# A kernel's planner learns of the port that VectorE and GpSimd share, and its loads are reordered

## Chip, cores and metric

One core of a Trainium2 chip runs the kernel. The metric is the device time of one execution in microseconds, the median of several runs on the same chip. Five engines work side by side and only semaphores order them: TensorE (PE in the profile; PEld is its weight load), VectorE (DVE), ScalarE (ACT), GpSimd (POOL), and SyncE (SP), which issues the DMA transfers.

## Reference

Three stages follow one another, all with float32 results. The attention has two batches of 8 heads, 576 positions and 64 dimensions; half of the heads look at the 32 positions before, the other half at every 32nd position. Its output, 1152 tokens of 512, goes through an MLP with a squared relu, whose weights come as float64, and then through four experts that are all computed and summed by weight.

```python
def _attn_ref(q, k, v):
    scores = scale * np.matmul(q, k.transpose(0, 1, 3, 2))
    mask_local = (rel >= 0) & (rel < stride)
    mask_strided = (rel >= 0) & (pos[None, :] % stride == pos[:, None] % stride)
    scores = np.where(masks[None, :, :, :], scores, -1000000000.0)
    attn = np.exp(scores - np.max(scores, axis=-1, keepdims=True))
    attn = attn / (np.sum(attn, axis=-1, keepdims=True) + 1e-09)
    return np.matmul(attn, v).astype(np.float32)

def _moe_ref(x, w_in, w_out):          # 512 -> 2048 -> 512
    h = np.maximum(x @ w_in, 0.0)
    return (h * h @ w_out).astype(np.float32)

def _moe2_ref(x, domain_probs, w1, w2):   # four experts, 512 -> 1024 -> 512
    p = domain_probs / (domain_probs.sum(-1, keepdims=True) + 1e-09)
    for e in range(E):
        out += p[:, e:e + 1] * (np.maximum(x @ w1[e], 0.0) @ w2[e])
```

## The kernel before

Products are made in three passes: each operand is split into a rounded upper part (ACT copies it, "hi") and a lower part (the difference, "lo"), and PE adds upper times upper, upper times lower and lower times upper (mm3, lines 617 to 619).

**Attention** works in 16 groups: six strided ones (lines 354 to 384) and ten local ones (lines 420 to 452). attend() gives each the same chain: loads of k, q and v by SP; scores on PE (L363 and L367, or L430 to L438); the maximum on DVE (L485); for local groups a negation (L492) and up to four exponentials on ACT with their sums (L490), for strided ones a subtraction (L495), one exponential (L496) and a sum (L497); then L498 and L499 on DVE; the normalisation on POOL (L500); transposes on PE (L372 or L442); a copy on ACT (L480); values on PE (L384 or L452); the x tile's upper part on ACT (L509) and its lower part on DVE (L513). Six groups form the startup, seven come "second", three "third". Local groups fill the first half of an x tile's 512 features, strided ones the second.

**The MLP** runs in 48 steps over three blocks of 384 tokens, 128 hidden features a step. A step's first products come in four quarters (features in the order 2, 3, 0, 1), so the first two need the strided groups alone. ACT and DVE make relu, square and the two parts (L650 to L660); two steps later the second products follow. The first eight steps take block 0, the next eight block 1.

**Weights** of this MLP arrive as float64, in 16 units of two halves (512 KB each, L568). ACT scales the upper words (L575), DVE shifts (L580), puts in the sign (L584) and the low bits (L589), ACT makes the upper part (L595), POOL the lower (L599). Expert weights are float32 and need only L595 and L599, the latter on DVE. The **experts** fill the span from about 240 us on; some products are combined so that seven stand for eight, and POOL builds sums of weights for that (L776 to L788).

**What orders the work** is Plan (class at the top). Each task names its engine with a cost in ns, what it follows, a rank, and buffers that it takes from rings and frees. run() plays the program through with these costs: an engine that falls idle takes the ready task of lowest rank whose buffers are there. What comes out is one fixed order for every engine and for SP's loads; on the chip each engine goes through its list and waits by semaphores. Ranks are counted in ns: due(n) for a step of the MLP, less CONV for the conversion of weights first used there, less FETCH for their load; for attention a start plus R_MAX, R_EXP, R_NORM, R_T, R_V, R_X along the chain. When PE has nothing before its first MLP task, it multiplies zeros (warm, L961). The rings are small: 3 raw weights, 2 of each middle tile, 10 finished units, 4 each of q, k and v, 3 of p.

```python
    def pool(n):
        return int(n * 2.05) + 190
    def dma(nbytes):
        return int(nbytes / 357) + 60
            lo_engines = {"pool": pool(n)} if wide_ else {"dve": dve(n)}
            t = plan.add(lo_engines, lo, after=[t], rank=rank + R_LO, ...)
```

Of the kernel before, what the change touches and what calls it, by code (L numbers as in the profile page):

```python
# [16 lines left out]
P = 128  # L17
# [22 lines left out]
class Plan:  # L40
# [7 lines left out]

    SAME, CROSS, DMA = 100, 200, 2200
# [13 lines left out]
    def add(self, engines, emit, after=(), rank=0, take=(), free=(), adds=(), behind=None, quiet=False, tenses=(), relaxes=()):  # L63
# [5 lines left out]
        t.quiet, t.tenses, t.relaxes = quiet, tenses, relaxes  # L69
        self.tasks.append(t)  # L70
        return t

    def run(self):
# [21 lines left out]
        while done < len(self.tasks):  # L95
# [25 lines left out]
            for e in ready:  # L121
                while idle[e] and ready[e]:
                    held, got = [], None
                    while ready[e]:
# [20 lines left out]
                    order.append((now, len(order), got.emit, e))  # L145
                    push(got.end, "end", got)
# [15 lines left out]
def tile_attention_mlp_experts(ctx: ExitStack, tc: tile.TileContext, a, out):  # L162
# [48 lines left out]
    NP = 3  # L211
    NQ = 4
    NPT = 2
# [25 lines left out]
    plan.ring("v", many(at, "v", NQ, [P, 512]))  # L239
# [12 lines left out]
    def mm_r(n):  # L252
        return int(n / 2.4) + 3

    def mm_s(n):
        return int(n / 2.4) + 13
# [9 lines left out]

    def dma(nbytes):
        return int(nbytes / 357) + 60
# [17 lines left out]
    IN, IN7, OUT = 3 * KD * mm_s(TB), 42 * mm_s(TB), 9 * mm_s(DM)  # L286
# [172 lines left out]
    attention_done = []  # L459

    def attend(g, rank, rings):
# [3 lines left out]
        for what, nbytes in zip("kqv", g.bytes):  # L465
            loads.append(plan.add({"dma": dma(nbytes)}, lambda e, w=what: g.load(env, w), rank=rank - 5000, take=[(env, what, [what])]))
# [17 lines left out]
        t = plan.add({"pe": g.cost_s}, lambda e: g.scores(env), after=[t_cb, t_go, *loads[:2]], rank=rank, take=[(env, "S", rings)], free=[(env, "q"), (env, "k")])  # L484
        t = plan.add({"dve": dve(n)}, lambda e: nc.vector.tensor_reduce(out=stat(0), in_=view(env["S"], g.cols), op=ALU.max, axis=AX.X), after=[t], rank=rank + R_MAX, take=[(env, "st", ["st"])])  # L485
        if g.units <= 4:
# [5 lines left out]
            t = plan.add({"dve": 90}, lambda e: nc.vector.tensor_scalar(out=stat(0), in0=stat(0), scalar1=-SCALE, scalar2=None, op0=ALU.mult), after=[t], rank=rank + R_MAX + 300)  # L492
            t = plan.add({"act": g.units * 317}, each, after=[t], rank=rank + R_EXP, take=[(env, "p", ["p"])], free=[(env, "S")])
# [4 lines left out]
        t = plan.add({"dve": 80}, lambda e: nc.vector.tensor_scalar(out=stat(1), in0=stat(1), scalar1=1e-9, scalar2=None, op0=ALU.add), after=[t], rank=rank + R_EXP + 1000)  # L498
# [23 lines left out]
    for k, g in enumerate(startup):  # L522
        attend(g, BASE + EACH * k, ["bank_a", "bank_y"])
    second = [Local(0, 3), Local(0, 4)] + [Strided(1, j) for j in range(3)] + [Local(1, 0), Local(1, 1)]
    for k, g in enumerate(second):
        attend(g, START - AHEAD + k * (due(half) - START - END2) // len(second), ["bank_a"])
    third = [Local(1, j) for j in (2, 3, 4)]
    for k, g in enumerate(third):
        attend(g, due(half) - AHEAD + k * (due(2 * half) - due(half) - END3) // len(third), ["bank_a"])
# [26 lines left out]
    for u in sorted(when, key=lambda x: when[x]):  # L556
# [4 lines left out]
        rank = when[u] - (CONV0 if soon else CONV)  # L561
        for j in range(2):
# [41 lines left out]
            if wide_:  # L604
                t = plan.add({"act": act(n)}, small, after=[t], rank=rank, take=[(env, "mid", ["mid"])])
                t = plan.add({"dve": dve(n // 2)}, shift, after=[t], rank=rank + 500, take=[(env, "val", ["val"])])
                t = plan.add({"dve": dve(n)}, sign, after=[t], rank=rank + 700, free=[(env, "mid")])
                t = plan.add({"dve": dve(n)}, low, after=[t], rank=rank + 1200, free=[(env, "raw")])
            t = plan.add({"act": act(n)}, hi, after=[t, chain["w"]], rank=rank + 2000, take=[(w_env[u], "w", ["w"])] if j == 0 else [], quiet=not wide_)
# [441 lines left out]
```

## Time and profile before

| | us |
|---|---|
| runs of the kernel (3): median, lowest, highest | 647.59, 647.18, 648.01 |
| profiled execution: time, span from first to last instruction | 647.54, 645.8 |
| PE busy, share of span | 631.5, 98% |
| VectorE busy | 360.8, 56% |
| ScalarE busy | 235.6, 36% |
| GpSimd busy | 105.9, 16% |
| granted TensorE clock, mean | 0.997 |

A span is cut into stretches and engines are compared within one; shares of the whole span mix a crowded beginning with a long stretch in which only PE matters. A matmul's time in a row is its latency; matmuls follow one another at about half of it. "Idle before" is time in which that engine stood still until the named one released it.

### The profile page before, as it was taken

Reading aid. Unit: us, or ns where it says so; the run is one execution under the profiler, and the core shown is the slowest. Engines: PE = TensorE matmul, PEld = TensorE weight load, DVE = VectorE, ACT = ScalarE, POOL = GpSimd, SP = SyncE. Lnnn points to the kernel's source line nnn. Section 1 sums busy time; section 2 is a strip of 40 time slices with the busy share of each in tenths; the row PEclk is TensorE's granted clock in tenths of the full one; section 3 lists DMA queues with packets and bytes.
Section 4 is the critical chain, followed back from the end, with each engine's and each line's share of the span. In section 5 each row is a group of like instructions: output and inputs, shape, how many; then the busy total and the mean of one; then the engine's idle time right before and its main releaser. Section 6 shows DMA issues by size and latency. Waiting matters only on the chain.

```text
span 645.8 us, 9891 instructions
## 1 busy us (share of the span) xinstructions
PE 631.5 (98%) x3868; PEld 580.2 (90%) x3868; DVE 360.8 (56%) x664; ACT 235.6 (36%) x527; POOL 105.9 (16%) x119
## 2 busy tenths in 40 slices
PE   7998999999999999999999999999999999999997
PEld 4777889999999999999999999999999999999997
DVE  4898886288623264945557415557324557643512
ACT  2956675354423244522333312333212333321110
POOL 2435341033100000030112000113001012400000
PEclk9998999999999999999999999999999999999999
DMA  8976434034300023231133301123301222100201
GB/s 276 265 228 179 150 127 131 0 100 145 98 1 1 1 65 98 72 91 38 38 94 136 89 1 50 63 90 110 81 1 50 81 82 97 33 2 0 98 2 49
DMA packets 28990, 53.51 MB, mean 83 GB/s; under 512 B 4432, under 2 KB 10000, under 8 KB 28944
## 3 DMA queue, kind: packets, MB, share of 16 engines
q1 hardware_dynamic: 28944, 52.89, 26.7%
q8 instruction: 30, 0.49, 0.3%
q14 instruction: 16, 0.13, 0.1%
HBM read 50.52 MB, written 2.36 MB: 82 GB/s over the span
## 4 chain that ended last, share of the span: by engine, by line
PE 88%; DVE 5%; ACT 2%; DMA 2%; issue 1%; POOL 1%; SPq 1%; DVEq 0%; ACTq 0%; POOLq 0%
PE bh L617 14%; PE bh L618 14%; PE bh L619 14%; PE by L835 8%; PE by L836 8%; PE by L834 8%; PE by L617 5%; PE by L619 4%; PE by L618 4%; PE ba L836 2%; PE ba L835 2%; PE ba L834 2%; DVE val L580 1%; DVE val L589 1%; DVE val L584 1%
## 5 line engine op out<-in xcount | busy, mean ns | idle before, releaser
L617 PE MATMUL bh<-x,w 128*128 128x384 f32 x416 | 141.8, 341 | 1.7 <-DVE h L660 1.7
L619 PE MATMUL bh<-x,w 128*128 128x384 f32 x416 | 139.8, 336 | 0.0
L618 PE MATMUL bh<-x,w 128*128 128x384 f32 x416 | 139.7, 336 | 0.0
L872 DVE TENSOR_TENSOR c<-bh,c 128x384 f32<-128x384 f32 x80 | 43.1, 556 | 85.9 <-ACT c L885 58.4
L836 PE MATMUL by<-w,h 128*128 128x512 f32 (+1 forms) x232 | 89.0, 384 | 0.0
L835 PE MATMUL by<-w,h 128*128 128x512 f32 (+1 forms) x232 | 89.0, 384 | 0.0
L834 PE MATMUL by<-w,h 128*128 128x512 f32 (+1 forms) x232 | 88.5, 382 | 0.0
L617 PEld LDWEIGHTS bh<-x,w 128*128 128x128 f32 x416 | 78.5, 189 | 4.7 <-DVE h L660 3.2
L618 PEld LDWEIGHTS bh<-x,w 128*128 128x128 f32 x416 | 78.5, 189 | 1.0
L619 PEld LDWEIGHTS bh<-x,w 128*128 128x128 f32 x416 | 78.4, 188 | 0.0
L779 POOL TENSOR_TENSOR sf<-raw 128x256 f32<-128x256 f32 x16 | 12.1, 755 | 347.1 <-DMA raw<-in_w_dram 283.8
L617 PE MATMUL by<-h,w 128*128 128x384 f32 x192 | 65.5, 341 | 0.3 <-ACT h L657 0.3
L618 PE MATMUL by<-h,w 128*128 128x384 f32 x192 | 64.5, 336 | 0.6 <-DVE h L660 0.6
L619 PE MATMUL by<-h,w 128*128 128x384 f32 x192 | 64.6, 336 | 0.0
L599 POOL TENSOR_TENSOR w<-val,w 128x512 fp32r<-128x512 f32 x32 | 43.3, 1361 | 76.4 <-ACT w L595 73.9
L654 DVE SCALAR_TENSOR_TENSOR bh<-bh,r 128x384 f32<-128x384 f32 x48 | 27.0, 562 | 51.0 <-ACT r L650 51.0
L929 DVE SCALAR_TENSOR_TENSOR h<-bh,h 128x384 fp32r<-128x384 f32 x32 | 17.8, 557 | 64.0 <-ACT h L926 64.0
L904 ACT ACTIVATE h<-c 128x384 fp32r<-128x384 f32 x64 | 31.8, 518 | 54.6 <-DVE c L872 34.5
L836 PEld LDWEIGHTS by<-w,h 128*128 128x128 f32 x232 | 43.6, 188 | 8.5
L834 PEld LDWEIGHTS by<-w,h 128*128 128x128 f32 x232 | 43.6, 188 | 8.0
L835 PEld LDWEIGHTS by<-w,h 128*128 128x128 f32 x232 | 43.6, 188 | 8.1
L599 DVE TENSOR_TENSOR w<-raw,w 128x512 fp32r<-128x512 f32 x64 | 43.1, 696 | 9.3 <-ACT w L595 9.3
(122 smaller groups left out, 1039.2 us busy)
## 6 DMA issues: line engine op xcount, KB each, us to landing
raw<-in_w_dram SPq DMA_DIRECT2D x64, 256.0 KB, 2.7
raw<-in_wi_dram SPq DMA_DIRECT2D x16, 512.0 KB, 3.7
raw<-in_wo_dram SPq DMA_DIRECT2D x16, 512.0 KB, 3.6
raw<-in_w_dram SPq DMA_DIRECT2D x16, 512.0 KB, 3.6
out_dram<-acc SPq DMA_DIRECT2D x8, 256.0 KB, 2.1
v<-in_vs_dram SPq DMA_DIRECT2D x6, 256.0 KB, 4.4
v<-in_vl_dram SPq DMA_DIRECT2D x8, 192.0 KB, 3.8
k<-in_kl_dram SPq DMA_DIRECT2D x8, 160.0 KB, 4.5
```

The lines of the kernel that those rows point to most:

```text
L599: eng[e].tensor_tensor(out=w[:, 1, cs], in0=value(), in1=f32(w[:, 0, cs]), op=ALU.subtract)
L617: nc.tensor.matmul(dst, lhsT=wh, rhs=xh, start=start, stop=False)
L618: nc.tensor.matmul(dst, lhsT=wh, rhs=xl, start=False, stop=False)
L619: nc.tensor.matmul(dst, lhsT=wl, rhs=xh, start=False, stop=stop)
L654: nc.vector.scalar_tensor_tensor(out=h, in0=h, scalar=0.0, in1=env["r"], op0=ALU.max, op1=ALU.mult)
L779: nc.gpsimd.tensor_tensor(out=got(env["sf"])[:, 0], in0=part(env, 1, 0), in1=part(env, 1, 1), op=ALU.add)
L834: nc.tensor.matmul(o, lhsT=h[:, 0, ts], rhs=w[:, 0], start=start, stop=False)
L835: nc.tensor.matmul(o, lhsT=h[:, 0, ts], rhs=w[:, 1], start=False, stop=False)
L836: nc.tensor.matmul(o, lhsT=h[:, 1, ts], rhs=w[:, 0], start=False, stop=stop)
L872: return lambda e: nc.vector.tensor_tensor(out=got(c[key]), in0=c[bank][:, :TB], in1=got(c[other]), op=ALU.add)
L904: nc.scalar.activation(out=env["hid"][:, 0], in_=got(c[key]), func=AF.Relu)
L929: nc.vector.scalar_tensor_tensor(out=env["hid"][:, 1], in0=env["H"][:, :TB], scalar=0.0, in1=f32(env["hid"][:, 0]), op0=ALU.max, op1=ALU.s ...
```

## The change

The planner gets a common mark for the port: a task with port=True, and every task on GpSimd, starts only when no such task is running by the plan. port=True is given to the DVE instructions L492, L498, L580, L584, L589, L599 and, in the later stages, to the differences and lower parts that read two tiles of the on-chip buffer. A float64 weight's lower part may go to GpSimd or VectorE. Costs are new: loads at 310 bytes per ns, PE's 384 columns at the higher of the two old figures, a normalisation of its own. Ranks are new throughout, CONV most of all, and the startup's loads get a lead of 9000 instead of 5000 while later groups get 1775. The rings of v and p grow. The two halves of a wi unit are loaded in the other order, and a quarter product waits for the half that it reads, not for both. Scores of the second and third groups follow the transposes of the group three before. In the expert stage the hold on GpSimd's sums ends later.

```diff
+        self.shared = 0
...
+        t.quiet, t.tenses, t.relaxes, t.port = quiet, tenses, relaxes, port
...
-                        if not (t.quiet and e in self.tense) and all(any(self.rings[r] for r in rings) for _, _, rings in t.take):
+                        if not (t.quiet and e in self.tense or (t.port or e == "pool") and now < self.shared) and all(any(self.rings[r] for r in rings) for _, _, rings in t.take):
...
+                    if got.port or e == "pool":
+                        self.shared = got.end
...
-    START, STEP, WITH, URGENT = 22863, 3902, 2300, 6004
+    START, STEP, WITH, URGENT = 16764, 7401, 1796, 5606
...
-    EACH = 3300
-    AHEAD = 4582
-    END2 = 7000
-    END3 = 12767
+    EACH = 3285
+    AHEAD = 3550
+    END2 = 5361
+    END3 = 11947
     CONV0 = 7431
-    CONV = 9000
-    FETCH = 2019
-    WITH2 = 1082
+    CONV = 70240
+    CONV2 = 9000
+    FETCH = 1560
+    WITH2 = 542
...
-    R_MAX = 1500
-    R_EXP = 2200
-    R_NORM = 6589
-    R_T = 6622
-    R_V = 4414
+    R_MAX = 2415
+    R_EXP = 1898
+    R_NORM = 1629
+    R_T = 1668
+    R_V = 5078
     R_X = 8089
-    R_LO = 2600
-    R_OUT = 1960
+    R_LO = 1232
+    R_OUT = 2590
...
-    NP = 3
+    NP = 5
     NQ = 4
+    NV = 6
+    LEAD0, LEAD = 9000, 1775
...
-    plan.ring("v", many(at, "v", NQ, [P, 512]))
+    plan.ring("v", many(at, "v", NV, [P, 512]))
...
     def mm_r(n):
-        return int(n / 2.4) + 3
-
-    def mm_s(n):
         return int(n / 2.4) + 13
...
+    def norm(n):
+        return int(n * 1.9) + 70
+
     def dma(nbytes):
-        return int(nbytes / 357) + 60
+        return int(nbytes / 310) + 60
...
-            loads.append(plan.add({"dma": dma(nbytes)}, lambda e, w=what: g.load(env, w), rank=rank - 5000, take=[(env, what, [what])]))
+            loads.append(plan.add({"dma": dma(nbytes)}, lambda e, w=what: g.load(env, w), rank=rank - lead, take=[(env, what, [what])]))
...
-        t = plan.add({"pe": g.cost_s}, lambda e: g.scores(env), after=[t_cb, t_go, *loads[:2]], rank=rank, take=[(env, "S", rings)], free=[(env, "q"), (env, "k")])
+        t = plan.add({"pe": g.cost_s}, lambda e: g.scores(env), after=[t_cb, t_go, *loads[:2], *(transposed[-3:-2] if len(rings) == 1 else [])], rank=rank, take=[(env, "S", rings)], free=[(env, "q"), (env, "k")])
...
-        t = plan.add({"pool": pool(n)}, lambda e: eng[e].tensor_tensor(out=view(env["p"]), in0=view(env["p"]), in1=wide(1), op=ALU.mult), after=[t], rank=rank + R_NORM, free=[(env, "st")])
+        t = plan.add({"pool": norm(n)}, lambda e: eng[e].tensor_tensor(out=view(env["p"]), in0=view(env["p"]), in1=wide(1), op=ALU.mult), after=[t], rank=rank + R_NORM, free=[(env, "st")])
         t = plan.add({"pe": g.cost_t}, lambda e: g.transposes(env), after=[t, t_ci], rank=rank + R_T, take=[(env, "T", rings)], free=[(env, "p")])
+        transposed.append(t)
...
-        rank = when[u] - (CONV0 if soon else CONV)
-        for j in range(2):
+        rank = when[u] - (CONV0 if soon else CONV if wide_ else CONV2)
+        for j in (1, 0) if kind == "wi" else (0, 1):
...
-                t = plan.add({"dve": dve(n // 2)}, shift, after=[t], rank=rank + 500, take=[(env, "val", ["val"])])
+                t = plan.add({"dve": dve(n // 2)}, shift, port=True, after=[t], rank=rank + 500, take=[(env, "val", ["val"])])
...
-            lo_engines = {"pool": pool(n)} if wide_ else {"dve": dve(n)}
-            t = plan.add(lo_engines, lo, after=[t], rank=rank + R_LO, free=[(env, "val") if wide_ else (env, "raw")], quiet=not wide_)
+            lo_engines = {"pool": pool(n), "dve": dve(n)} if wide_ else {"dve": dve(n)}
+            t = plan.add(lo_engines, lo, port=True, after=[t], rank=rank + R_LO, free=[(env, "val") if wide_ else (env, "raw")], quiet=not wide_)
...
-                previous = plan.add({"pe": 3 * mm_r(TB)}, product, after=[previous if pos else None, *x_ready[b, (0, 1) if kk < 2 else (2, 3)], *w_ready[u]], rank=due(n) + pos * PE_SLICE, ...)
+                previous = plan.add({"pe": 3 * mm_r(TB)}, product, after=[previous if pos else None, *x_ready[b, (0, 1) if kk < 2 else (2, 3)], w_ready[u][kk < 2]], rank=due(n) + pos * PE_SLICE, ...)
...
-                    t = on_act(hi, [t], take=[(env, "hid", ["hid"])], relaxes=("act",) if key == "c22" else ())
+                    t = on_act(hi, [t], take=[(env, "hid", ["hid"])], relaxes=("act", "pool") if key == "c22" else ())
```

## Rows read from the trace of the kernel before

**Rows 1.** Stretches of the span: busy us of each engine (instructions), granted clock, DMA

```profile
core 0: us, PE busy (x) PEld busy (x) DVE busy (x) ACT busy (x) POOL busy (x), PEclk, DMA share, GB/s
...
26.61:110.00 83.39, 78.30 (x746) 69.41 (x743) 73.29 (x145) 53.98 (x146) 33.36 (x29) 0.98 0.55 170
110.00:165.00 55.00, 54.39 (x311) 53.39 (x310) 35.38 (x55) 24.73 (x50) 14.92 (x11) 1.00 0.28 86
165.00:645.80 480.80, 477.47 (x2497) 443.45 (x2495) 237.00 (x421) 144.02 (x288) 49.01 (x65) 1.00 0.19 57
```

**Rows 2.** Waits of PE: line waited for, us in total, times, longest

```profile
PE ba L433 <- DVE x L513: 1.9, 1, 1.9
PE bh L617 <- DVE h L660: 1.7, 3, 0.9
...
PE ba L372 <- POOL p L500: 0.7, 1, 0.7
PE by L618 <- DVE h L660: 0.6, 1, 0.6
```

**Rows 3.** Stretches again, columns as in the first group: startup, and around the lower clock

```profile
0.00:5.66 5.66, 4.67 (x12) 1.64 (x12) 0.11 (x1) 1.28 (x1) 1.65 (x7) 1.00 0.59 176
5.66:26.61 20.95, 16.69 (x312) 12.33 (x311) 15.01 (x44) 11.54 (x45) 6.94 (x7) 1.00 1.01 299
...
60.50:64.00 3.50, 3.50 (x13) 3.50 (x13) 2.49 (x11) 2.71 (x11) 1.80 (x3) 0.52 0.28 109
```

**Rows 4.** Lines of VectorE and GpSimd: busy us, mean ns; or ns min/median/max

```profile
L584 DVE SCALAR_TENSOR_TENSOR val<-mid,val 128x512 uint32<-128x512 uint32 x32 | 24.6, 769 | 0.5
L580 DVE TENSOR_SCALAR val<-mid 128x512 uint32<-128x512 uint32 x32 | 23.3, 728 | 7.6 <-ACT mid L575 6.0 <-POOL w L599 1.2
...
L599 POOL TENSOR_TENSOR w<-val,w 128x512 fp32r<-128x512 f32 x31 | 42.0, 1363 | 73.5 <-ACT w L595 71.1 <-PE by L619 2.5
...
L599 DVE TENSOR_TENSOR w<-raw,w 128x512 fp32r<-128x512 f32 x64 | 43.1, 696 | 9.3 <-ACT w L595 9.3
...
L580 DVE TENSOR_SCALAR val<-mid x32: 406/424/1570, 14.9 to 162.7; 128x512 uint32<-128x512 uint32 x32
...
L584 DVE SCALAR_TENSOR_TENSOR val<-mid,val x32: 673/682/1684, 15.6 to 163.8; 128x512 uint32<-128x512 uint32 x32
...
L492 DVE TENSOR_SCALAR st<-st x10: 111/158/1276, 15.6 to 89.2; 128x4 f32<-128x4 f32 x8, 128x2 f32<-128x2 f32 x2
```

**Rows 5.** Timeline of the startup: start us, us, engine, line, [idle before <-releaser]

```profile
11.63 1.78 POOL L500 TENSOR_TENSOR p<-p,st 128x432 f32<-128x432 f32 x2 [9.45 <-DVE st L498]
...
14.17 0.66 ACT L575 ACTIVATE mid<-raw 128x512 f32<-128x512 f32 x1 [3.66 <-DMA raw<-in_wi_dram]
14.73 0.43 ACT L496 ACTIVATE p<-p 128x288 f32<-128x288 f32 x1
...
15.02 0.88 PE L438 MATMUL ba<-k,q 64*64 64x96 f32 x16 [0.95 <-DMA q<-in_ql_dram]
...
15.82 0.66 PE L372 MATMUL by<-ident,p 128*128 128x128 f32 x4
...
26.61 0.44 PE L617 MATMUL bh<-x,w 128*128 128x384 f32 x1
```

**Rows 6.** Waits of SP, which issues the loads: us in total, times, longest

```profile
SPq L424 <- PE ba L384: 10.1, 4, 4.5
```

**Rows 7.** Timeline: the last local group of block 0, from scores to its first user

```profile
18.09 0.88 PE L438 MATMUL ba<-k,q 64*64 64x96 f32 x16
...
19.82 1.25 DVE L492 TENSOR_SCALAR st<-st 128x4 f32<-128x4 f32 x1
...
23.89 0.35 ACT L490 ACTIVATE p<-ba,st 128x96 f32<-128x96 f32 x1
...
26.77 0.83 POOL L500 TENSOR_TENSOR p<-p,st 128x384 f32<-128x384 f32 x1 [1.86 <-DVE st L499]
...
29.90 0.64 PE L442 MATMUL by<-ident,p 128*96 128x128 f32 x4
...
33.74 0.45 PE L617 MATMUL bh<-x,w 128*128 128x384 f32 x1
```

More of the change, by code (lines that the diff above doesn't have):

```diff
@@ L58, in __init__, with add @@
         self.tense = set()
+        self.shared = 0
     def ring(self, name, tiles):
         self.rings[name] = list(tiles)
-    def add(self, engines, emit, after=(), rank=0, take=(), free=(), adds=(), behind=None, quiet=False, tenses=(), relaxes=()):
+    def add(self, engines, emit, after=(), rank=0, take=(), free=(), adds=(), behind=None, quiet=False, tenses=(), relaxes=(), port=False):
         t = Plan.Task()
@@ L490, in each @@
                     nc.scalar.activation(out=env["p"][:, cs], in_=env["S"][:, cs], func=AF.Exp, scale=SCALE, bias=stat(0)[:, u : u + 1], accum_out=stat(1)[:, u : u + 1])
-            t = plan.add({"dve": 90}, lambda e: nc.vector.tensor_scalar(out=stat(0), in0=stat(0), scalar1=-SCALE, scalar2=None, op0=ALU.mult), after=[t], rank=rank + R_MAX + 300)
-            t = plan.add({"act": g.units * 317}, each, after=[t], rank=rank + R_EXP, take=[(env, "p", ["p"])], free=[(env, "S")])
+            t = plan.add({"dve": 90}, lambda e: nc.vector.tensor_scalar(out=stat(0), in0=stat(0), scalar1=-SCALE, scalar2=None, op0=ALU.mult), port=True, after=[t], rank=rank + R_MAX + 300)
+            t = plan.add({"act": g.units * 330}, each, after=[t], rank=rank + R_EXP, take=[(env, "p", ["p"])], free=[(env, "S")])
         else:
@@ L604, in tile_attention_mlp_experts @@
             if wide_:
-                t = plan.add({"act": act(n)}, small, after=[t], rank=rank, take=[(env, "mid", ["mid"])])
-                t = plan.add({"dve": dve(n // 2)}, shift, after=[t], rank=rank + 500, take=[(env, "val", ["val"])])
-                t = plan.add({"dve": dve(n)}, sign, after=[t], rank=rank + 700, free=[(env, "mid")])
-                t = plan.add({"dve": dve(n)}, low, after=[t], rank=rank + 1200, free=[(env, "raw")])
-            t = plan.add({"act": act(n)}, hi, after=[t, chain["w"]], rank=rank + 2000, take=[(w_env[u], "w", ["w"])] if j == 0 else [], quiet=not wide_)
+                t = plan.add({"act": act(n) + 60}, small, after=[t], rank=rank, take=[(env, "mid", ["mid"])])
+                t = plan.add({"dve": dve(n // 2)}, shift, port=True, after=[t], rank=rank + 500, take=[(env, "val", ["val"])])
+                t = plan.add({"dve": dve(n)}, sign, port=True, after=[t], rank=rank + 700, free=[(env, "mid")])
+                t = plan.add({"dve": dve(n)}, low, port=True, after=[t], rank=rank + 1200, free=[(env, "raw")])
+            t = plan.add({"act": act(n)}, hi, after=[t, chain["w"]], rank=rank + 2000, take=[(w_env[u], "w", ["w"])] if u not in w_ready else [], quiet=not wide_)
             chain["w"] = t
-            lo_engines = {"pool": pool(n)} if wide_ else {"dve": dve(n)}
-            t = plan.add(lo_engines, lo, after=[t], rank=rank + R_LO, free=[(env, "val") if wide_ else (env, "raw")], quiet=not wide_)
+            lo_engines = {"pool": pool(n), "dve": dve(n)} if wide_ else {"dve": dve(n)}
+            t = plan.add(lo_engines, lo, port=True, after=[t], rank=rank + R_LO, free=[(env, "val") if wide_ else (env, "raw")], quiet=not wide_)
             w_ready.setdefault(u, []).append(t)
@@ L644, in tile_attention_mlp_experts @@
                 freed = [(w_env[u], "w")] if pos == 3 and last_use[u] == n else []
-                previous = plan.add({"pe": 3 * mm_r(TB)}, product, after=[previous if pos else None, *x_ready[b, (0, 1) if kk < 2 else (2, 3)], *w_ready[u]], rank=due(n) + pos * PE_SLICE, take=[(env, "H", ["bank_h"])] if pos == 0 else [], free=freed, adds=[("bank_y", [spare])] if n == 0 and pos == 0 else ())
+                previous = plan.add({"pe": 3 * mm_r(TB)}, product, after=[previous if pos else None, *x_ready[b, (0, 1) if kk < 2 else (2, 3)], w_ready[u][kk < 2]], rank=due(n) + pos * PE_SLICE, take=[(env, "H", ["bank_h"])] if pos == 0 else [], free=freed, adds=[("bank_y", [spare])] if n == 0 and pos == 0 else ())
             t = previous
@@ L750, in tile_attention_mlp_experts @@
             rank = base + (n * hk + k) * 1000
-            t = plan.add({"dve": dve(TB)}, diff, after=[*x2_wide.values(), t_late, *t_sums], rank=rank)
+            t = plan.add({"dve": dve(TB)}, diff, port=True, after=[*x2_wide.values(), t_late, *t_sums], rank=rank)
             t_sums.append(t)
             t = plan.add({"act": act(TB)}, hi, after=[t, previous], rank=rank)
-            t_ready[n].append(plan.add({"dve": dve(TB)}, lo, after=[t], rank=rank))
+            t_ready[n].append(plan.add({"dve": dve(TB)}, lo, port=True, after=[t], rank=rank))
     def open_last(e):
@@ L801, in tile_attention_mlp_experts @@
             h = plan.add({"act": act(2 * hk * P)}, hi, after=[t], rank=rank + 2000 + 500 * k, quiet=True)
-            s_ready[u].append(plan.add({"dve": dve(2 * hk * P)}, lo, after=[h, *s_ready[u]], rank=rank + 2000 + 500 * k, free=[(env, "sf")] if k == 1 else [], quiet=True))
+            s_ready[u].append(plan.add({"dve": dve(2 * hk * P)}, lo, port=True, after=[h, *s_ready[u]], rank=rank + 2000 + 500 * k, free=[(env, "sf")] if k == 1 else [], quiet=True))
     nt = TB // P
@@ L862, in seven @@
                     ready = [*(s_ready[un] if x[0] == "s" else w_ready[u]), *(t_ready[y[1]] if y[0] == "t" else [x2_ready[pair[y[2]], y[1] * hk + k] for k in range(hk)])]
-                    return on_pe(3 * hk * mm_s(TB), product, t_in, ready, take=taken(bank, "bank_h"), **more)
+                    return on_pe(3 * hk * mm_r(TB), product, t_in, ready, take=taken(bank, "bank_h"), **more)
                 def on_act(emit, after, c=c, **more):
@@ L955, in tile_attention_mlp_experts @@
                         freed += [(w_env[u], "w")] if last_part[u] == (e_, two) else []
-                t = on_pe(3 * mm_s(cols), second_product(env, u, i % 2, y, t_, cs, new, stop), t_out, [env["ready"], *w_ready[u]], take=[(y, "y", ["bank_y", "bank_a"])] if new else [], free=freed)
+                t = on_pe(3 * mm_r(cols), second_product(env, u, i % 2, y, t_, cs, new, stop), t_out, [env["ready"], *w_ready[u]], take=[(y, "y", ["bank_y", "bank_a"])] if new else [], free=freed)
                 if stop:
```

25 lines of the change are left out of this document (12 added, 13 removed).

## The prediction

> **What bounds the kernel now.** I cut the span by TensorE first, because a kernel in which one engine is busy for 98% can only be shortened where that engine waits or does work of another kind. In the stretches of [rows 1] the last, from 165 us to the end, keeps PE busy for 477.5 of 480.8 us, and the one before it for 54.4 of 55.0. What is left to gain lies ahead of 110 us: the startup of 26.61 us, up to the first product of the MLP, then 83.4 us in which the attention of the later groups, the conversion of the float64 weights and the first MLP steps run together. VectorE is busy there for 73.3 of 83.4 us, and ACT and POOL are far from full. So the second look is at who ends PE's waits. [rows 2] name VectorE first: 1.9 us in one wait for an x tile, 1.7 and 0.6 us for the lower part of a hidden tile; POOL's normalisation costs 0.7. That is 4.9 us. PE is the bound, VectorE decides when it is fed. The third look is at the granted clock: right behind the 1.9 us wait, in 60.5 to 64.0, it stands at 0.52, the lower of the two levels (1.2 GHz). At half speed 3.5 us hold 1.8 us of work, so 1.7 us are lost [rows 3]. PE's own list of waits therefore understates VectorE's part: 4.9 + 1.7 = 6.6 us.
>
> The fourth look is at why VectorE is late. The shift of a weight (line 580) takes 424 ns in the median and up to 1570, the sign (line 584) 682 and up to 1684; their means are 728 and 769 [rows 4]. The long ones lie beside GpSimd's subtraction of line 599, which takes 1363 ns. Over 32 calls that is 32 x (728 - 424) = 9.7 us and 32 x (769 - 682) = 2.8 us: 12.5 us of VectorE in two lines, spent waiting for GpSimd. The planner of before puts such pairs side by side, since it takes them for independent.
>
> The last look is at the startup, where the order itself makes engines wait. GpSimd has normalised two strided groups by 13.41, but PE transposes them only at 15.82: the scores of a local group stand ahead in PE's order, and their q lands at 15.0 [rows 5]. ACT idles 3.66 us for the first raw weights and does that conversion ahead of an exponential, which starts at 14.73 [rows 5]. The queue of loads stands still for v tiles: the four v buffers are taken until PE's line 384 frees them, 10.1 us of waiting in four issues [rows 6].
>
> **The change, part by part.** *Startup.* It has six v and five p buffers, ranks the normalisation and the transposes about 5 us nearer to the scores (R_NORM 6589 to 1629, R_T 6622 to 1668), plans loads at 310 instead of 357 bytes per ns, and lets the first product wait for one half of the first weight unit alone. The loads of the startup, with both halves of that unit, are 4.66 MB by the tiles' shapes. The queue moves 299 GB/s with all its engines busy [rows 3]; at 176 GB/s until 5.66, 1.0 MB has come by then, and the rest takes 3.66 / 0.299 = 12.2 us, so all is there by 17.9. The last local group of token block 0 gates the third and fourth quarter of every step. In the trace its scores start at 18.09 and the product that needs its x tile starts at 33.74 [rows 7]. Loads do not move that 18.09 by much, so the gain has to come from the 15.7 us behind it, and in them three gaps are queueing: the negation takes 1.25 us beside GpSimd, where its like takes 0.16 (the median of line 492, [rows 4]; 1.1 us); the exponentials start at 23.89, 2.8 us after its end; and GpSimd is done with the normalisation at 26.77 + 0.83 = 27.60, but PE transposes at 29.90, 2.3 us later [rows 7]. Together 6.2 us. I take three quarters, because ACT stays crowded: 4.6, put down as **4.5 us**, which moves 33.74 to about 29. It counts in full, since PE has the scores of the next groups and the half products of the first two steps to fill the time, as now. Bounds: nothing, if PE is then stopped by weights, and 6.2.
>
> The Trainium skill's page "SBUF — State Buffer" (Summary: rules for kernel authors) has HBM loads run at about 358 GB/s. By that rate the loads would be there at 15.9, 2.0 us sooner, and the forecast would be 2.0 us lower; the trace has 299 with the engines full, and that decides.
>
> *The port.* Every VectorE instruction that the trace shows stretched gets a flag, and the planner starts none of them while GpSimd works, nor GpSimd while one of them runs. The lower part of a converted weight may go to either engine. GpSimd holds it for 1363 ns; VectorE's subtraction of the same shape has a mean of 696 [rows 4]. If half of the 32 go over, VectorE gains 16 x 0.70 = 11.1 us of work, loses most of 12.5 us of stalls in two lines alone, and GpSimd loses 21.8 us of work. VectorE's load stays about equal, but its stalls no longer fall on whatever is behind them. What is late behind VectorE is PE, by 6.6 us as above. I take two thirds of it away, **4.5 us**, since PE also waits where VectorE simply has much to do (88% busy in the second stretch). Bounds: 0, if the collisions come back, and 6.6, or 7.4 with some waits too small for the rows.
>
> The Trainium skill's same summary says of VectorE and GpSimd on that port that "the second one to issue fully blocks until the first finishes" and advises to schedule "whichever is off the critical path". That speaks against moving subtractions to VectorE, the engine that PE waits for; by that advice all 32 stay on GpSimd and 11.1 us of VectorE are spared. Rows weigh the other way: beside flagged work the 1363 ns are VectorE's loss too.
>
> *Weights first.* CONV goes from 9000 to 70240 for the float64 weights beyond the first three units, so each of their steps outranks all attention that is not done. A conversion is limited by three raw buffers and two of each middle tile, so only short instructions (0.4 to 0.7 us) get in front; I put **+0.4 us** for that and for PE changing sides more often. Below, this can give 0.5 by feeding steps sooner; above, see the third case.
>
> *The rest.* Two more memsets of p lie on GpSimd well ahead of its first work at 11.63 [rows 5]; cover gone, they would cost their half microsecond each. The rule that a later group's scores wait for the transposes three groups back holds no engine. The flags and the longer hold on GpSimd in the expert stage touch a stretch in which PE idles for 3.3 us of 480.8, mostly at its end [rows 1]: nothing, with slack of half of VectorE's time as cover.
>
> Sum: -4.5 - 4.5 + 0.4 = -8.6. The profiled execution took 647.54 (span 645.8 and 1.7 around it), which stands 0.05 below the median of the three runs, 647.59. 647.54 - 8.6 = 638.9, rounded to **639.0 us**.
>
> **The rivals.** *One term only.* The order of each engine is fixed when the kernel is built; if instructions drift by half a microsecond, GpSimd meets VectorE again and the waits stay; or the earlier start only brings PE sooner to weights that are not converted. For it: 12.5 us of stalls arose under a plan too. Against: plan and chip were apart there by a lock of 1.3 us that the plan did not have. One term of 4.5 lost gives 643.4. *It does not do what it says.* PE is the bound and the new order only moves its waits: 647.5. For it speaks PE's 94% in the second stretch [rows 1]. *Slower: conversions starve the attention.* The 16 halves of the first eight units cost VectorE about 1.8 us each (0.42 and twice 0.68, the third line taken as the second), half of them 0.7 more: 34 us of work that goes ahead of the seven middle groups. Those need all four engines in turn, 7 to 15 us each, and step 8 needs their x. Eight steps of 24 matmuls at 0.175 us (311 in 54.4 us, [rows 1]) are 34 us of PE; if the groups come 10 us late with no other product ready, PE stands for 9 us, and falls to the lower clock behind it as at 60.5, 2 us more. -8.6 + 11 = +2.4: 650.0. It decides once PE's new idle time passes 8.6 us. Against it: attention is PE's only filler there, and the conversions wait for loads of 512 KB each.
>
> **How the numbers follow.** Both terms: 0.52, its own range 633.5 to 643. One term: 0.25, 641.5 to 646. No change: 0.08. Slower: 0.15. About 0.2%, 1.3 us, is what a measurement can tell from no change. So faster 0.77, same 0.08, slower 0.15. The range starts at the bounds of both terms (-6.2 - 7.4 - 0.5, that is 633.4, put at 633.0) and reaches to 647.5, which leaves out the slower case and a little at the lower end.
>
> **What would show it.** Right: the first product starts near 21 to 23 and the product that waits for the local group near 29; line 580's mean falls below 500 ns; some 16 subtractions of line 599 are on VectorE; PE's waits for VectorE fall below 2.5 us and no half clock follows 60; the last 470 us do not differ. Wrong: line 580 keeps values of 1.5 us (the plan did not carry over); PE waits for x tiles or p for several us between 50 and 100 (starved attention); the first product moves but the moment from which PE is dense does not (the start was given back).

## Result and profile after

The changed kernel takes 642.47 us in the median of 9 runs (639.34 to 646.76) against 648.01 for the kernel before; the ratio is 0.991, interval 0.9885 to 0.9937, so it is faster by about 5.8 us. The forecast of 639.0, 8.6 us below the kernel before, promised more; its range held the result. The profiled execution took 641.69, with a span of 639.9, 5.9 less than before.

The stretches of the changed kernel, columns as in [rows 1]:

```profile
0.00:26.61 26.61, 23.25 (x331) 15.77 (x332) 15.64 (x46) 14.09 (x51) 8.09 (x15) 1.00 0.89 265
26.61:110.00 83.39, 80.16 (x761) 72.40 (x760) 71.94 (x161) 54.42 (x143) 14.08 (x14) 0.98 0.57 178
110.00:165.00 55.00, 55.00 (x319) 55.00 (x319) 37.51 (x67) 25.86 (x52) 3.90 (x3) 1.00 0.26 82
165.00:639.90 474.90, 471.45 (x2462) 437.52 (x2460) 235.91 (x416) 140.59 (x282) 48.72 (x64) 1.00 0.19 57
```

PE's waits of the changed kernel, the longest (line waited for, us in total, times, longest), which answer to [rows 2]:

```profile
PE ba L449 <- ACT p L497: 1.8, 1, 1.8
PE ba L445 <- DMA q<-in_ql_dram: 1.3, 1, 1.3
...
PE ba L370 <- ACT pt L487: 0.7, 1, 0.7
...
PE ba L440 <- DVE x L521: 0.3, 1, 0.3
PE by L626 <- DVE h L668: 0.2, 1, 0.2
```

VectorE is gone from the top: 0.5 us in the two rows shown that name it, against 4.2 of the 4.9 us in [rows 2]; only the first wait of all, for the zeros of warm(), is in both kernels as before, 1.0 us. The wait for q is not new: the kernel before has one, its largest row, which [rows 2] leave out and which lies in the startup.

```profile
PE ba L438 <- DMA q<-in_ql_dram: 2.4, 2, 1.4
```

The conversion's lines in the first 165 us (580, 584, 589 and 599 are 588, 592, 597 and 607 now; busy us, mean ns), which answer to [rows 4]:

```profile
L597 DVE SCALAR_TENSOR_TENSOR val<-raw,val 128x512 uint32<-128x512 uint32 x32 | 21.8, 687 | 0.3
L592 DVE SCALAR_TENSOR_TENSOR val<-mid,val 128x512 uint32<-128x512 uint32 x32 | 21.8, 685 | 0.2
L607 DVE TENSOR_TENSOR w<-val,w 128x512 fp32r<-128x512 f32 x25 | 18.5, 741 | 6.9 <-ACT w L603 6.6
L588 DVE TENSOR_SCALAR val<-mid 128x512 uint32<-128x512 uint32 x32 | 15.6, 487 | 2.0 <-ACT mid L583 1.8
...
L607 POOL TENSOR_TENSOR w<-val,w 128x512 fp32r<-128x512 f32 x7 | 9.6, 1377 | 55.4 <-ACT w L603 55.4
```

Of the kernel before, the third line, which puts in the low bits and which [rows 4] do not show:

```profile
L589 DVE SCALAR_TENSOR_TENSOR val<-raw,val 128x512 uint32<-128x512 uint32 x32 | 25.4, 794 | 0.3
```

The sign's mean is 685 where it was 769, the shift's 487 where it was 728, the low bits' 687 where it was 794. Together the three lines take 59.2 us of VectorE where they took 73.3. 25 of 32 subtractions went to VectorE.

To see where the time went I cut both traces at two events: the start of the 13th matmul of the MLP, the first that needs the local groups (the 33.74 of [rows 7]), and the start of the 193rd. The third line of each triple of matmuls counts them: four triples ahead of the first cut, 60 between the cuts. Kernel before, all engines, columns as in [rows 1]:

```profile
0.00:33.74 33.74, 28.49 (x432) 19.73 (x433) 21.37 (x62) 19.63 (x66) 11.35 (x18) 1.00 0.92 270
33.74:91.45 57.71, 52.62 (x517) 45.47 (x513) 52.17 (x104) 36.12 (x102) 24.18 (x21) 0.97 0.54 167
```

The changed kernel at the same events, and that count:

```profile
0.00:35.35 35.35, 29.43 (x431) 20.66 (x431) 22.15 (x63) 19.53 (x65) 11.04 (x18) 0.97 0.92 281
35.35:85.58 50.23, 49.56 (x495) 43.82 (x493) 45.18 (x106) 32.93 (x90) 9.38 (x9) 0.99 0.57 174
...
35.35:85.58 50.23, 20.21 (x60) 11.41 (x60) 0.99 0.57 174
```

The first stretch is 1.6 us longer, the second 7.5 us shorter. PE's idle time is 5.3 and then 5.1 us before, 5.9 and then 0.7 after. From the 193rd to the 577th matmul, first of the kernel before, then of the changed one:

```profile
91.45:160.80 69.35, 68.74 (x406) 67.38 (x406) 46.95 (x75) 33.71 (x69) 20.04 (x15) 1.00 0.33 102
...
85.58:154.74 69.16, 69.16 (x426) 68.43 (x425) 49.19 (x93) 36.88 (x81) 5.66 (x5) 1.00 0.31 101
```

Both take 69 us, and from there to the end both take 485. So the gain lies between 34 and 91 us. But the stretch between the first two cuts does not hold the same work in both kernels. Without the multiplied zeros, PE starts 410 matmuls ahead of the 13th in both; from there to the 193rd it starts 512 before and 492 after, and the 20 that are missing follow later. At the 577th every kernel of this document has started 1326. This is the cut at which times can be compared: 160.8 us before, 154.7 after, a gain of 6.1 us. From the 13th to the 577th PE's idle time falls from 5.7 to 0.7 us.

### The profile page after: what moved, and what is told of

Same layout as the page of the kernel before. It is cut to its first block, busy times and chain, and to the rows that moved or that the text cites. A ratio compares the mean times of both kernels' runs of the same rounds, so it can differ in the third digit from the quotient of the medians.

```text
span 639.9 us, 9860 instructions
## 1 busy us (share of the span) xinstructions
PE 629.9 (98%) x3867; PEld 580.7 (91%) x3867; DVE 361.0 (56%) x689; ACT 235.0 (37%) x527; POOL 74.8 (12%) x96
## 4 chain that ended last, share of the span: by engine, by line
PE 92%; DMA 4%; ACT 1%; SPq 1%; DVE 1%; issue 0%; ACTq 0%; DVEq 0%
PE bh L625 15%; PE bh L627 15%; PE bh L626 15%; PE by L843 8%; PE by L844 8%; PE by L842 8%; PE by L625 5%; PE by L626 5%; PE by L627 5%; PE ba L843 2%; PE ba L844 2%; PE ba L842 2%; DMA raw<-in_wo_dram 2%; DMA raw<-in_wi_dram 1%; DMA k<-in_ks_dram 1%; PE ba L459 1%
## 5 line engine op out<-in xcount | busy, mean ns | idle before, releaser
L662 DVE SCALAR_TENSOR_TENSOR bh<-bh,r 128x384 f32<-128x384 f32 x48 | 27.1, 564 | 49.6 <-ACT r L658 49.4
L937 DVE SCALAR_TENSOR_TENSOR h<-bh,h 128x384 fp32r<-128x384 f32 x32 | 17.8, 558 | 59.9 <-ACT h L934 59.9
L658 ACT ACTIVATE r<-bh 128x384 f32<-128x384 f32 x48 | 23.5, 489 | 66.5 <-PE bh L627 66.1
```

The source lines that it names most:

```text
L658: nc.scalar.activation(out=env["r"], in_=env["H"][:, :TB], func=AF.Relu, scale=1.0 / WSCALE)
L662: nc.vector.scalar_tensor_tensor(out=h, in0=h, scalar=0.0, in1=env["r"], op0=ALU.max, op1=ALU.mult)
L937: nc.vector.scalar_tensor_tensor(out=env["hid"][:, 1], in0=env["H"][:, :TB], scalar=0.0, in1=f32(env["hid"][:, 0]), op0=ALU.max, op1=ALU.s ...
```

## Experiments

Ratios are to runs of the kernel before on the same chip. The cuts are counted in the records of each profile as above. A profile is of one execution, whose time stands beside it and can lie some us from the median. The last column is the time at the lower clock ahead of the 577th matmul.

| run | ratio, interval | profiled, us | 13th at | 13th to 193rd | 577th at | lower clock |
|---|---|---|---|---|---|---|
| before | | 647.54 | 33.7 | 57.7 | 160.8 | 3.4 |
| changed | 0.991, 0.9885 to 0.9937 | 641.69 | 35.4 | 50.2 | 154.7 | 3.4 |
| b_port | 1.0007, 0.999 to 1.0025 | 648.40 | 40.3 | 51.1 | 161.3 | 10.2 |
| a_noport | 1.0002, 0.9983 to 1.0021 | 649.83 | 36.7 | 57.0 | 163.0 | 6.8 |
| a_poollo | 0.9921, 0.9888 to 0.9955 | 646.79 | 39.3 | 51.5 | 160.1 | 10.2 |
| b_start | 1.0042, 1.0017 to 1.0066 | 654.26 | 39.0 | 60.0 | 167.3 | 17.1 |
| after_again | 0.9922, 0.9898 to 0.9945 | 641.94 | 35.6 | 50.2 | 155.0 | 3.4 |
| a_fill | 0.988, 0.986 to 0.990 | 641.84 | 35.8 | 50.0 | 154.9 | 0 |
| a_act | 0.9901, 0.9878 to 0.9925 | 645.00 | 37.8 | 51.1 | 158.0 | 10.2 |
| a_fill_act | 0.9888, 0.9867 to 0.9909 | 641.49 | 35.8 | 49.6 | 154.5 | 0 |
| a_late | 0.9936, 0.9913 to 0.996 | 645.37 | 37.6 | 53.2 | 158.6 | 10.2 |
| a_conv9 | 0.9919, 0.9889 to 0.995 | 641.92 | 34.8 | 51.1 | 155.0 | 3.4 |
| b_port_fill | 0.998, 0.996 to 1.000 | 645.91 | 39.0 | 49.8 | 158.8 | 0 |
| b_fill | 0.999, 0.9969 to 1.001 | 647.12 | 33.4 | 57.7 | 160.4 | 0 |

**b_port: the port alone in the old kernel.** The marks on the conversion and on L492 and L498, the choice of engine, and the rule in run():

```diff
+ ... (t.port or e == "pool") and now < self.shared ...
+                    if got.port or e == "pool":
+                        self.shared = got.end
-            lo_engines = {"pool": pool(n)} if wide_ else {"dve": dve(n)}
+            lo_engines = {"pool": pool(n), "dve": dve(n)} if wide_ else {"dve": dve(n)}
```

> The kernel before with the planner's knowledge of the port and the choice of engine for converted lower parts, and nothing else of the change: old ranks, costs, buffers and load order. Port theory (the gain of the change, about 6 us, comes from VectorE no longer standing beside GpSimd): 641 to 644 us, line 580's mean below 500 ns, PE's waits after the start at 1 to 2 us instead of 6.6. Order theory (the gain comes from new ranks, costs and loads): VectorE's stalls go as well, but PE still waits as often, 646 to 649 us.

649.35 us: no difference. The second stretch is nearly as short as in the changed kernel, but the 13th matmul comes 6.6 us later than in the kernel before. b_port, columns as in [rows 1]:

```profile
0.00:40.30 40.30, 32.50 (x467) 22.73 (x467) 25.29 (x70) 20.55 (x67) 8.92 (x15) 0.92 0.84 255
40.30:91.36 51.06, 48.58 (x443) 43.29 (x444) 46.25 (x101) 32.78 (x95) 14.29 (x13) 0.97 0.56 166
```

In part this is work that changed sides. b_port starts 443 matmuls ahead of the 13th and 443 between the cuts, where the kernel before has 410 and 512. At the 577th, with the same work done, it stands at 161.3 us against 160.8. Its three conversion lines, for 31 of the 32 halves:

```profile
L587 DVE SCALAR_TENSOR_TENSOR val<-mid,val 128x512 uint32<-128x512 uint32 x31 | 22.5, 735 | 0.5 <-issue 0.2
L592 DVE SCALAR_TENSOR_TENSOR val<-raw,val 128x512 uint32<-128x512 uint32 x31 | 21.1, 687 | 0.2
L583 DVE TENSOR_SCALAR val<-mid 128x512 uint32<-128x512 uint32 x31 | 16.3, 527 | 0.8 <-POOL p L503 0.5
```

That is 59.9 us, as little as in the changed kernel. VectorE's stalls are gone and PE's idle time up to the 577th is not: 10.3 us, where the kernel before has 10.9; 2.4 us of PE's waits still name VectorE. One piece of the new order stands in VectorE's timeline (start, us): it waited for 2.3 us, in its fixed order, for the tiny load of the experts' probabilities, which nothing needs before the experts.

```profile
29.34 0.19 DVE L317 TENSOR_REDUCE pe_s<-pe 128x9 f32<-128x36 f32 x1 [2.27 <-DMA pe<-in_pe_dram]
```

PE waited for 1.9 us a little later, until 31.6, and 6.8 us at the lower clock follow. This is the form of my order theory, 0.35 us above its range: the stalls go, and PE waits as before.

**a_noport: the changed kernel without the knowledge.**

```diff
- ... not (t.quiet and e in self.tense or (t.port or e == "pool") and now < self.shared) and ...
+ ... not (t.quiet and e in self.tense) and ...
```

> The changed kernel whose planner ignores the port mark; lower parts may still go to either engine. Port theory: stalls of line 588 come back (mean 650 to 750 ns), PE's waits rise by 3 to 5 us, 645 to 648 us. Order theory: 641 to 643.5 us as the changed kernel.

648.75 us: all of the gain is gone. a_noport between its cuts, and its conversion lines:

```profile
36.65:93.61 56.96, 52.68 (x524) 45.46 (x522) 52.25 (x114) 36.98 (x104) 14.72 (x13) 0.98 0.53 155
...
L592 DVE SCALAR_TENSOR_TENSOR val<-mid,val 128x512 uint32<-128x512 uint32 x32 | 28.4, 886 | 0.4
L597 DVE SCALAR_TENSOR_TENSOR val<-raw,val 128x512 uint32<-128x512 uint32 x31 | 23.4, 755 | 0.3
L588 DVE TENSOR_SCALAR val<-mid 128x512 uint32<-128x512 uint32 x32 | 16.2, 505 | 5.0 <-ACT mid L583 4.9
```

PE idles 4.3 us there instead of 0.7, and the sign has a mean of 886 ns. The shift did not go back (505); the collisions fell on other lines than the expectation said, 68.0 us on the three. Of PE's waits three name VectorE again:

```profile
PE bh L625 <- DVE h L668: 2.7, 4, 1.4
...
PE ba L459 <- DVE p L502: 1.2, 1, 1.2
PE ba L449 <- DVE x L521: 1.0, 1, 1.0
```

So the rule gives nothing without the rest of the change (b_port), and the rest gives nothing without the rule: the gain takes both. Which part of the rest it takes, no run shows. The rest holds the new ranks, and these may have been chosen with the rule in place; no run gives the planner without the rule ranks of its own, so a_noport may also be slow because its ranks do not fit it.

**a_poollo: every lower part on GpSimd.**

```diff
-            lo_engines = {"pool": pool(n), "dve": dve(n)} if wide_ else {"dve": dve(n)}
+            lo_engines = {"pool": pool(n)} if wide_ else {"dve": dve(n)}
```

> The changed kernel with every converted lower part on GpSimd again, the planner still knowing the port. If the move of subtractions to VectorE is what matters: VectorE may not work on marked instructions for 1.3 us beside each of 32, conversions slow down, 645 to 648 us. If only the knowledge of the port matters: 641 to 644 us.

643.53 us, not to be told from the changed kernel, though a difference of 2 or 3 us would not show in these intervals. Its conversion lines:

```profile
L597 DVE SCALAR_TENSOR_TENSOR val<-raw,val 128x512 uint32<-128x512 uint32 x32 | 27.0, 848 | 0.2
L592 DVE SCALAR_TENSOR_TENSOR val<-mid,val 128x512 uint32<-128x512 uint32 x32 | 25.3, 794 | 0.3
L588 DVE TENSOR_SCALAR val<-mid 128x512 uint32<-128x512 uint32 x32 | 16.5, 515 | 4.4 <-ACT mid L583 2.5 <-POOL w L607 1.6
```

VectorE's stalls are back, 68.8 us on the three lines against 59.2 in the changed kernel and 68.0 in a_noport, and the gain is still there. With b_port that makes four cases: with the stalls gone 642.5 us (changed) and 649.4 (b_port), with them back 643.5 (a_poollo) and 648.8 (a_noport). The time does not follow the sum of the stalls. What the rule gives must then lie in the order that the planner makes with it, or in where the stalls fall, and these runs do not separate the two.

**b_start: the startup's parts alone in the old kernel.** R_NORM, R_T, NP, NV, dma(), the order of the halves and the half wait, as in the change.

```diff
-    R_NORM = 6589
-    R_T = 6622
+    R_NORM = 1629
+    R_T = 1668
...
-        return int(nbytes / 357) + 60
+        return int(nbytes / 310) + 60
```

> The kernel before with the startup's parts alone: six v and five p buffers, normalisation and transposes at the new ranks, loads planned at 310 bytes per ns, the halves of the first unit in the other order with a product waiting for one half only. By the startup term of my prediction: 4.5 us faster, 643 us. Rival, from the changed kernel's trace, in which the product that waits for the local groups came no earlier (35.4 against 33.7): nothing gained, 646.5 to 649 us.

651.29 us, slower by 0.4% and 2.3 us above the rival's range. The term for the startup is not there; the 13th matmul is 5 us late, with 453 matmuls ahead of it instead of 410, and the profile, of a run of 654.26, shows 17 us at the lower clock, 6.8 from 25.9 and 10.2 from 60.0.

**after_again, a_fill, a_act, a_fill_act: the clock, and ACT's order.** The first is the changed kernel. a_fill lets PE multiply zeros where it waits, fourteen of twenty onto two sums that are open anyway, so that nothing changes in them:

```diff
+    def zeros(e, n, spare_=False):
+        for k in range(n):
+            if spare_:
+                nc.tensor.matmul(spare, lhsT=idle, rhs=spread(idle, 4), start=True, stop=True)
+            else:
+                nc.tensor.matmul(use[k % 2]["H"][:, :TB], lhsT=idle, rhs=spread(idle, 3), start=False, stop=False)
```

a_act swaps one pair on ACT:

```diff
-                t = plan.add({"act": act(n) + 60}, small, after=[t], rank=rank, ...)
+                t = plan.add({"act": act(n) + 60}, small, after=[t, *exps[2:3]], rank=rank, ...)
```

> The changed kernel once more, unedited, as the measure for its variants on the same chip: 641 to 643 us. If the spread of its times is the lower clock, then times go with the mean granted clock of each run: near 639 to 640 us where that is 1.000, 643 and more below 0.993.

> The changed kernel with products of zeros at three places where PE waits in the startup: six ahead of the first local group's scores, ten (added to two open accumulations) ahead of the seventh group's transposes, four ahead of the ninth group's scores; nothing else moves. Clock theory (a wait of PE between 25 and 33 us is followed by a stretch at the lower clock, and this costs the changed kernel some 3 us in the median run): mean clock 0.998 to 1.000, 639 to 640.5 us, spread below 3 us. Rival (PE is short of operands there and the clock only follows): unchanged 641.5 to 643.

> The changed kernel with one swap in ACT's order: the exponential of the third strided group goes ahead of the first scaling of raw weights, which waits for its load. My startup term named this wait (ACT idle for 3.7 us before, 4.0 after the change). If it decides when the first product starts: that moves from 24.2 to about 22, and the time falls by 1 to 2 us against the changed kernel. Rival: the later local group decides, nothing changes (within 0.7 us).

> Both edits. If both theories hold they add up: 637.5 to 639.5 us. If only the clock counts: 639 to 640.5.

Medians 643.35, 641.27, 642.61 and 641.52 us. after_again has a mean clock of 0.994 over its runs, a_fill 0.999, and its times spread over 2.2 us instead of 3.9; its median is 2.1 us lower, though above the 639 to 640.5 expected. None of after_again's six runs had a clock of 1.000; the one below 0.993 took 645.67, as expected. In the profiled run of the changed kernel PE waits 1.8 us ahead of 31.2 and 0.7 ahead of 32.6, and the clock falls to its lower level at 33.1; of a_fill's timeline:

```profile
30.97 1.80 PE L475 MATMUL bh<-idle 128*128 128x384 bf16 x10
32.60 0.60 PE L449 MATMUL ba<-ident,p 128*96 128x128 f32 x4
33.04 0.81 PE L475 MATMUL bh<-idle 128*128 128x384 bf16 x4
```

and no lower clock until the last microsecond. The changed kernel in that place, columns as in [rows 1]:

```profile
33.10:36.50 3.40, 3.40 (x52) 3.18 (x47) 2.26 (x5) 1.39 (x3) 1.27 (x1) 0.51 0.90 284
```

The swap on ACT gave nothing that can be told from the spread, alone or on top of the zeros, and a_fill_act lies above both of its ranges. a_act's profile has 10.2 us at the lower clock and its first product at 26.5, not at 22. In the profiles of a_fill and a_fill_act, which have none ahead of the 577th, the first product stands at 25.8 and the 13th at 35.8 in both. So that wait of ACT does not set the start.

**a_late: loads of the last local group first.**

```diff
-        rank = when[u] - (CONV0 if soon else ...)
+        rank = when[u] - (3000 if u == ("wi", 0, 0) else CONV0 if soon else ...)
```

> The changed kernel with the first weight unit's conversion ranked 4.4 us later, so that its loads go behind those of the last local group of block 0 (in the changed kernel they moved ahead, and that group's scores went from 18.1 to 20.8). If those loads hold up the start: the group's scores go back to about 18, the 13th product of the MLP moves from 35.4 to 31 to 33, the time falls by 2 to 4 us against the changed kernel's 642 to 643. Rival (ACT and PE decide, the group only waits elsewhere): 13th product within 1 us of 35.4, time within 1 us.

645.17 us: if anything slower than the changed kernel. The edit did what it was for, and more. The scores of block 0's last local group start at 16.85 where the changed kernel has 20.75, and yet the lower part of its x tile is done at 36.1 where the changed kernel has 33.1 (a_late's timeline; the changed kernel's stands below):

```profile
16.85 0.88 PE L445 MATMUL by<-k,q 64*64 64x96 f32 x16
...
35.66 0.42 DVE L521 TENSOR_TENSOR x<-by,x 128x256 fp32r<-128x256 f32 x1
```

The first product came at 30.5 instead of 24.2, its weights being converted later, and the 13th at 37.6, with 10.2 us at the lower clock in this profile. So the loads of that group do not decide when the 13th starts.

**a_conv9: conversions no longer outrank attention** (CONV 70240 to 9000).

> The changed kernel with CONV back at 9000, so that conversions no longer outrank the attention. If the weights' precedence is part of the gain: the 192nd product comes 2 to 4 us later than 85.4, 645 to 647 us. If it costs, as my slower case has it: 639 to 641. If it is neutral: 641.5 to 643.5.

642.91 us: neutral within 2 us either way, so neither a large part of the gain nor the threat of my slower case.

**b_port_fill and b_fill: zeros in the old kernel,** with b_port's edit and without. As zeros() above, ahead of the tasks that their expectations name.

> The run with the port knowledge alone (b_port, 649.4 us, its profile with 10.2 us at the lower clock in the startup and the 13th product at 40.3 instead of 33.7), now with products of zeros in PE's three waits there: ten ahead of the seventh group's transposes, four ahead of the ninth group's scores, six ahead of the 13th product. Theory (the port gives some 6 us behind the 13th product, and the old order loses as much ahead of it, mostly by waits and the lower clock behind them): mean clock 0.998 or more, 645.5 to 647.5 us, faster than the kernel before. Rival (the port knowledge is worth nothing by itself): 648 to 650 us as without the zeros.

> The kernel before with ten products of zeros, added to two open accumulations, ahead of the scores for which PE waits 1.9 us at 57; nothing else. If that wait brings the lower clock at 60.5 here too: mean clock about 0.999, 647 to 648 us, 0.5 to 1.5 below the kernel before on the same chip. It sets the measure for what holding the clock is worth without the change.

647.40 and 647.73 us. b_port_fill's mean clock is 0.9985 where b_port had 0.993, its 13th matmul comes at 39.0, and its ratio falls from 1.0007 to 0.998, at the edge of what can be told. b_fill cannot be told from the kernel before, which took 647.90 there; the 0.5 to 1.5 us that I expected are not seen. Neither profile has the lower clock ahead of the 577th matmul, which starts at 158.8 and 160.4 us. In one profile each, that makes 1.6 us for the rule in the old order with the clock held, far from the 6 that I looked for.

## Why the prediction was right, and for which part by luck

**The reading of the bound held, the reason behind it is not shown.** PE is the bound, and VectorE decided when it was fed: PE's waits for it fell from 4.2 to 0.5 us, and without the rule they are back. That VectorE was late because of its stalls beside GpSimd is the step that the runs do not bear out: b_port removes the stalls without a gain, and a_poollo has the gain with the stalls. They show that the rule is needed under the new ranks, 0.9% or 5.9 us between a_noport and the changed kernel, with some 2 us either way.

**The port's term had about the right size.** I put 4.5 us, two thirds of 6.6, since PE also waited where VectorE merely had much to do. From the 13th to the 577th matmul PE idles 5.0 us less, and a_noport's 5.9 lies between 4.5 and the upper bound of 7.4. The 7.5 us between the first two cuts are no measure of it: they hold 20 matmuls fewer and 2.2 us less at the lower clock. VectorE is as full there as before, 52.2 of 57.7 us and then 45.2 of 50.2. That half of the subtractions would move was a guess (25 did), and the term did not depend on it: a_poollo has the gain with none moved. With the path unproven, the size is partly luck.

**The startup's term failed: 4.5 us forecast, 1.6 the other way measured.** The failing step is the reading of [rows 7], from which the 6.2 us of queueing gaps were taken. They are not the rows of one group. Block 0 needs the first three local groups, all of the startup; the scores at 18.09, the negation at 19.82, the exponentials at 23.89 and the normalisation at 26.77 belong to the seventh group, whose tokens 384 to 511 lie in block 1. The bank tells it: the code gives the later groups bank `ba` alone, and the last scores of full size before the first product lie in `by`. The kernel before (start, us), the group that block 0 waits for:

```profile
21.79 0.88 PE L438 MATMUL by<-k,q 64*64 64x96 f32 x16
...
25.98 0.37 ACT L490 ACTIVATE p<-by,st 128x96 f32<-128x96 f32 x1
...
33.07 0.41 DVE L513 TENSOR_TENSOR x<-by,x 128x256 fp32r<-128x256 f32 x1
```

The changed kernel's timeline (start, us), with the same group's scores at 20.75 and its x tile at 32.64:

```profile
14.29 0.66 ACT L583 ACTIVATE mid<-raw 128x512 f32<-128x512 f32 x1 [4.04 <-DMA raw<-in_wi_dram]
...
20.75 0.88 PE L445 MATMUL ba<-k,q 64*64 64x96 f32 x16
...
31.23 0.61 PE L449 MATMUL ba<-ident,p 128*96 128x128 f32 x4 [1.82 <-ACT p L497]
...
32.58 0.34 PE L370 MATMUL ba<-cb 128*128 128x432 bf16 x1 [0.74 <-ACT pt L487]
32.64 0.42 DVE L521 TENSOR_TENSOR x<-ba,x 128x256 fp32r<-128x256 f32 x1
32.85 1.52 PE L374 MATMUL ba<-k,q 64*54 64x54 f32 x32
...
34.30 1.12 PE L459 MATMUL ba<-pt,v 96*64 96x64 f32 x16
35.35 0.69 PE L625 MATMUL bh<-x,w 128*128 128x384 f32 x1
```

From its scores to the end of its x tile this group takes 11.7 us before and 12.3 after: it begins 1.0 us earlier and ends 0.4 earlier, and nothing of 6.2 us was there to be had. "Loads do not move that 18.09 by much" thus spoke of another group, as does the 18.1 in a_late's expectation. The 13th matmul comes later all the same, since PE reaches it 2.3 us after the tile: its fixed order puts the seventh group's transposes first, for which it waits 1.8 us (31.23), then the ninth group's scores after 0.7 us and the seventh's values, both in part at the lower clock. The kernel before has the same tasks ahead of that matmul and reaches it 0.3 us after the tile.

ACT's wait for raw weights is 4.0 us where it was 3.7 [rows 5]. ACT, which works on every link of every chain, is nearly full from there on in both kernels. The stretch from 14.3 to 33 us, columns as in [rows 1], first of the changed kernel:

```profile
14.30:33.00 18.70, 15.28 (x250) 12.14 (x249) 15.69 (x46) 16.49 (x62) 5.33 (x6) 1.00 0.94 285
```

and of the kernel before:

```profile
14.30:33.00 18.70, 16.69 (x272) 13.33 (x274) 15.40 (x46) 16.35 (x62) 7.33 (x8) 1.00 0.96 272
```

ACT is busy for 16.5 and 16.4 of 18.7 us, so making one chain shorter needs another to wait. That ACT is what holds the start is argued from these rows and not shown by a run: a_act and a_late changed orders there and won nothing.

**The +0.4 for weights first** cannot be told from nothing (a_conv9 is neutral). **The rivals:** "one term only", 643.4, describes the time that came, and it was the port's term that stayed. The slower case did not come; the new waits of PE are 2.5 us in the startup and not 9. b_start shows that a slower kernel was near, by the startup's order and the clock.

**The sums.** The profiled spans differ by 5.9 us, the medians by 5.5, where I had 8.6: what was forecast for the port came, what was forecast for the startup did not. That the range held the result with one of its two terms read from another group's rows is owed to its width of 14.5 us. Of the signs named in advance, those of the port came (line 588 at 487 ns, 0.5 us of PE's waits for VectorE, an unchanged end), though one value of 1.4 us of line 588 is left, which I had named as a sign of being wrong. Those of the startup did not come (24.2 for 21 to 23, 35.4 for 29), and the lower clock did not go but moved from 60.5 to 33.1.

## What to carry to other kernels

A planner that writes a fixed order should know of a resource that two engines exclude each other from: here the gain was gone without that knowledge, and the knowledge alone gave nothing. To show that a removed cost was the cause, bring the cost back alone; a_poollo did, and the gain stayed. Before gaps in one chain are counted as a saving, make sure that all rows are of one group, by its bank and the code, and that the engines on it are idle then. And a new order should be compared at an event ahead of which the same work is done, such as the 577th matmul: between the 13th and the 193rd b_port looks 6.6 us faster with 69 matmuls fewer.

## What was not expected of the hardware

The spread of the changed kernel's times is largely the granted clock: its nine runs go from 639.34 us at a mean clock of 1.000 to 646.76 at 0.988. In the kernel before it is less so: its runs at 1.000 on one chip go from 647.01 to 649.66. In three profiles here a PE wait of 1.8 to 1.9 us was followed within 2 us of its end by 3.4 to 6.8 us at 1.2 GHz (the kernel before at 60.5, the changed one at 33.1, b_port at 31.6). The length of one wait does not decide it: in a_act one of 1.9 us ended at 8.2 and the lower clock came only at 14.0, behind another of 2.4, while in a_late one of 1.5 us, until 12.0, was followed by it at 12.2. Products of zeros in such waits went with a clock of 1.000 in the profiles of b_fill and b_port_fill and 0.999 in that of a_fill, and over all runs with a mean of 0.9986 for b_fill against 0.9968 for the kernel before on that chip. a_fill has the lowest median of all: 641.27 us, 0.988 of the kernel before, where the unedited changed kernel on the same chip has 0.9922; the two intervals just overlap.
